# Batches 0 and 1 with one form of softmax, batch 1 divided after its product with V, masks as a transfer of their own, and a new listed order

## The chip, the cores and the metric

One core of one Trainium2 chip runs the whole kernel: TensorE (PE) for matmuls, VectorE (DVE), ScalarE (ACT) and GpSimd (POOL) for the element work, SyncE (SP) for issuing transfers. The metric is device microseconds of one execution; a median over several runs is given.

## What is computed

Attention with a sliding window over q, k, v of 8 batches, 8 heads, 576 positions and 64 features; heads 0 to 3 look at the 32 last positions, heads 4 to 7 at every fourth of the last 128. The 4,608 tokens x 512 features that come out go through a feed-forward layer whose activation is a quotient of polynomials.

```python
scores = scale * np.matmul(q, k.transpose(0, 1, 3, 2))        # q, k: (8, 8, 576, 64)
scores = np.where(masks, scores, -1e9)                        # window 32; heads 4..7 dilated by 4
attn = np.exp(scores - np.max(scores, axis=-1, keepdims=True))
attn = attn / (np.sum(attn, axis=-1, keepdims=True) + 1e-09)
x = np.matmul(attn, v).transpose(0, 2, 1, 3).reshape(8 * 576, 512)
h = x @ w_in                                                  # 512 -> 2048
P = a[0] + a[1] * h + a[2] * h**2 + a[3] * h**3
Q = 1.0 + np.abs(b[0]) * np.abs(h) + np.abs(b[1]) * h**2
out = (P / (Q + 1e-6)) @ w_out                                # 2048 -> 512
```

## The kernel before

**Feed-forward tiles.** PE's main work is 144 tiles, each of 512 tokens by 128 of the 2,048 hidden features (`Tile`, line 907). All operands are split in a high and a low part, so a product is three matmuls: a tile's h is 12 matmuls of 128x512 into one of two banks `h`, and its four outputs are 3 each, added up over 16 tiles in four banks `out`. In between lies a chain over the engines: |h| on ACT (`a`), Q's linear part `r`, the product `a<-r,a` on DVE or POOL, P by two DVE steps on `t`, the quotient by `ln` and `exp` on ACT (into the bank of h), three DVE products (`g1`, `g0`, `g2`, the last two on `a` and the bank), and the split into `gh` and `gl`. Tiles 0 to 7 are chunk 0 (batch 0's x), 8 to 23 chunk 1 (batch 1's x), 24 to 31 the rest of chunk 0, 32 on chunk 2. Weights arrive as 64-bit words and are converted on the core: scale on ACT, a low word on POOL or ACT, a join on DVE (`wi_f<-wi_f,wi_raw`), a high part and a low part (`wi<-wi_f,wi`).

**Attention.** 48 units n = 6 b + u run beside the tiles (`Unit`, line 382). A unit is 48 score matmuls into bank `pair`, a mask, a softmax, transposes, 48 products with V and the move of the results into x's layout, split into `xh` and `xl`. Batch 0 keeps its scores in bands and has banks `pair_A`, `pair_B` beside `pair`; batch 1 transposes by PE; both have the mask put into the bank by PE with a bf16 identity, ahead of the scores. From batch 2 on mask and transposes go over DVE and DRAM. Results of batches 1 on go by `y` to DRAM and back as `z`. `x0` must be whole before tile 0, `x1` before tile 8, `x2` before tile 32. The products of unit n use the bank in which the scores of unit n + 2 come next.

**Three forms of softmax.** `KIND` says which form a unit of batches 0 and 1 takes. Form 0: row maximum and subtraction on DVE, exp on ACT, sum, reciprocal on DVE, product on POOL or DVE. Form 1 (unit 4): six ACT instructions read the bank and sum up as well (`exp_bank`, line 451). Form 2 (units 6 to 11): DVE takes the negated maximum, PE adds it to the bank by two fp32 products with the identity (`sub_pe`, line 471; four matmul instructions), ACT reads the bank, and six ACT copies scale the result (`norm`, line 491). Units 4 and 5 form `xl0` by PE, which subtracts `xh0` in the bank by a negated identity (`less_hi`, line 631, with `LESS`).

**What sets the order.** Every operation is entered in `Plan` (line 127) with costs per engine and dependencies. `ORDER` (line 70) lists operation numbers in the order they are placed, with an engine's letter where it is chosen by hand; before, the list reaches about tile 30. What isn't listed is placed by `run` (line 195): the operation that can start first on any engine names the engine, and of those that can start there within 200 ns the one with the lowest due rank goes (`DUE`, `LATE`, `SLACK`). Instructions of an engine then run in that order. PE also gets some bf16 matmuls in its idle time at the very start (`keep_busy`).

Of the kernel before, what the change touches and what calls it, by code (L numbers as in the profile page):

```python
# [20 lines left out]
P = 128  # L21
# [5 lines left out]
BOTH = {"ACT": 375, "DVE": 465}  # L27
# [3 lines left out]
KIND = [0, 0, 0, 0, 1, 0] + [2] * 6  # L31
LESS = [0, 0, 0, 0, 1, 1]
# [246 lines left out]
def tile_attention_moe(  # L279
# [102 lines left out]
    class Unit:  # L382
# [280 lines left out]
        def plan(self, by, tags):  # L663
# [19 lines left out]
            if start:  # L683
                mask_users.append(sc)
# [582 lines left out]
```

## Time and profile before

| what | us |
|---|---|
| median of 3 runs (888.88 to 891.14) | 889.17 |
| the profiled execution's span | 887.4 |
| PE busy | 873.8 (98%) |
| DVE busy | 716.1 (81%) |
| ACT busy | 666.1 (75%) |
| POOL busy | 504.7 (57%) |
| first matmul of tile 0 | 35.78 |

The span is that of one profiled execution and is read for where time goes; the median is the time that counts. PE's granted clock is 1.0 in all stretches. Durations of matmuls overlap in the timeline, since they are pipelined, so the start of the next one is read rather than the end of one.

### The profile page before, as it was taken

Reading aid. Unit: us, or ns where it says so; the run is one execution under the profiler, and the core shown is the slowest. Engines: PE = TensorE matmul, PEld = TensorE weight load, DVE = VectorE, ACT = ScalarE, POOL = GpSimd, SP = SyncE. Lnnn points to the kernel's source line nnn. Section 1 sums busy time; section 2 is a strip of 40 time slices with the busy share of each in tenths; the row PEclk is TensorE's granted clock in tenths of the full one; section 3 lists DMA queues with packets and bytes.
Section 4 is the critical chain, followed back from the end, with each engine's and each line's share of the span. In section 5 each row is a group of like instructions: output and inputs, shape, how many; then the busy total and the mean of one; then the engine's idle time right before and its main releaser. Section 6 shows DMA issues by size and latency. Waiting matters only on the chain.

```text
span 887.4 us, 20762 instructions
## 1 busy us (share of the span) xinstructions
PE 873.8 (98%) x7991; PEld 710.8 (80%) x7991; DVE 716.1 (81%) x1280; ACT 666.1 (75%) x1108; POOL 504.7 (57%) x467
## 2 busy tenths in 40 slices
PE   7999999999999999999999999999999999999998
PEld 4777888888878888888888888888888888888886
DVE  6899999998899978878888788888766666667665
ACT  4999988776567877777767777767777788777773
POOL 4477867767555655556555464655554456444442
PEclk9999999999999999999999999999999999999999
DMA  9976451337534424433544344323310020001001
GB/s 345 346 247 205 178 216 31 106 110 229 168 121 131 139 76 149 135 113 115 157 144 140 107 133 163 113 90 98 119 27 1 1 71 1 1 1 48 1 1 47
DMA packets 85187, 102.64 MB, mean 116 GB/s; under 512 B 37216, under 2 KB 62560, under 8 KB 85088
## 3 DMA queue, kind: packets, MB, share of 16 engines
q1 hardware_dynamic: 85088, 101.32, 35.1%
q8 instruction: 62, 1.02, 0.5%
q14 instruction: 37, 0.30, 0.1%
HBM read 74.42 MB, written 26.87 MB: 114 GB/s over the span
## 4 chain that ended last, share of the span: by engine, by line
PE 90%; DVE 6%; ACT 1%; issue 1%; DMA 1%; POOL 0%; SPq 0%; DVEq 0%; ACTq 0%; POOLq 0%
PE out L337 43%; PE h L337 41%; PE pair L337 6%; DVE a L346 1%; DVE h L346 1%; DMA qk<-in_qk_dram 1%; ACT p L340 1%; DVE a L343 1%; DVE t L343 0%; DVE t L346 0%; DVE sm L485 0%; DVE y L567 0%; DVE wo_f L346 0%; DVE mx L445 0%; PE pair_B L337 0%
## 5 line engine op out<-in xcount | busy, mean ns | idle before, releaser
L337 PE MATMUL h<-xh,wi 128*128 128x512 f32 x1136 | 374.3, 391 | 1.5 <-DVE a L346 1.4
L337 PE MATMUL out<-gh,wo 128*128 128x512 f32 x1136 | 354.0, 393 | 0.0
L349 POOL TENSOR_TENSOR a<-r,a 128x512 f32<-128x512 f32 x130 | 168.6, 1297 | 232.1 <-ACT r L340 224.5
L337 PEld LDWEIGHTS h<-xh,wi 128*128 128x128 f32 x1136 | 213.2, 188 | 47.9 <-DVE a L346 2.5
L346 DVE SCALAR_TENSOR_TENSOR a<-a,h 128x512 f32<-128x512 f32 x280 | 191.2, 683 | 69.2 <-POOL gl L349 36.9
L337 PEld LDWEIGHTS out<-gh,wo 128*128 128x128 f32 x1136 | 210.6, 188 | 45.1
L337 PE MATMUL out<-gl,wo 128*128 128x512 f32 x568 | 221.3, 390 | 0.0
L337 PE MATMUL h<-xl,wi 128*128 128x512 f32 x568 | 221.2, 389 | 0.0
L349 POOL TENSOR_TENSOR gl<-a,gh 128x512 fp32r<-128x512 f32 x133 | 175.9, 1322 | 56.7 <-ACT gh L340 56.0
L340 ACT ACTIVATE a<-h 128x512 f32<-128x512 f32 x140 | 83.6, 597 | 104.7 <-PE h L337 101.9
L343 DVE TENSOR_TENSOR t<-t,h 128x512 f32<-128x512 f32 x142 | 97.2, 684 | 62.8 <-ACT t L340 62.0
L340 ACT ACTIVATE r<-a,ln_bias 128x512 f32<-128x512 f32 x141 | 100.9, 716 | 31.7 <-POOL a L349 27.4
L337 PEld LDWEIGHTS out<-gl,wo 128*128 128x128 f32 x568 | 106.7, 188 | 22.4
L337 PEld LDWEIGHTS h<-xl,wi 128*128 128x128 f32 x568 | 106.7, 188 | 21.9
L340 ACT ACTIVATE t<-h,na_t 128x512 f32<-128x512 f32 x142 | 108.5, 764 | 3.1 <-PE h L337 3.1
L340 ACT ACTIVATE h<-r,exp_bias 128x512 f32<-128x512 f32 x142 | 98.0, 690 | 16.7 <-DVE t L346 10.7
L346 DVE SCALAR_TENSOR_TENSOR t<-t,na_t,h 128x512 f32<-128x512 f32 x142 | 105.8, 745 | 4.2
L346 DVE SCALAR_TENSOR_TENSOR h<-t,na_t,h 128x512 f32<-128x512 f32 x142 | 106.1, 747 | 0.0
L340 ACT ACTIVATE r<-a,ab_t 128x512 f32<-128x512 f32 x120 | 97.9, 816 | 3.9
L340 ACT ACTIVATE gh<-a 128x512 fp32r<-128x512 f32 x130 | 81.8, 629 | 24.0 <-PE out L337 19.1
L349 POOL TENSOR_TENSOR xl<-z,xh 128x256 fp32r<-128x256 f32 (+5 forms) x60 | 44.1, 753 | 2.4 <-ACT xh L340 1.3
L349 POOL TENSOR_TENSOR p<-p,sm 128x384 f32<-128x384 f32 x36 | 30.7, 853 | 17.0 <-DVE sm L489 16.0
(131 smaller groups left out, 687.1 us busy)
## 6 DMA issues: line engine op xcount, KB each, us to landing
qk<-in_qk_dram SPq DMA_DIRECT2D x48, 448.0 KB, 5.0
v<-in_vp_dram SPq DMA_DIRECT2D x42, 384.0 KB, 3.8
out_dram<-os SPq DMA_DIRECT2D x36, 256.0 KB, 2.5
wi_raw<-in_w_in_dram SPq DMA_DIRECT2D x16, 512.0 KB, 7.6
wo_raw<-in_w_out_dram SPq DMA_DIRECT2D x16, 512.0 KB, 6.4
results<-y SPq DMA_DIRECT2D x42, 192.0 KB, 2.0
z<-results SPq DMA_DIRECT2D x168, 48.0 KB, 2.1
turned<-u SPq DMA_DIRECT2D x36, 192.0 KB, 2.0
```

What stands on the lines that cost most here:

```text
L337: pin(nc.tensor.matmul(o, lhs, rhs, start=start, stop=stop, skip_group_check=free))
L340: pin(nc.scalar.activation(o, i, func, **kw))
L343: pin(nc.vector.tensor_tensor(o, x, y, op))
L346: pin(nc.vector.scalar_tensor_tensor(o, x, s, y, op0, op1))
L349: pin(nc.gpsimd.tensor_tensor(o, x, y, op))
```

## The change

One form of softmax (0) stays. Batch 0's units keep sum, reciprocal and product; batch 1's units leave the sum and the division out (`defer`). V of batches 1 to 7 is stored with a 65th column of ones, so that the products give the sum of each row beside the result, and `rescale` divides in the bank, on DVE, before the results are turned. Masks and coefficients have a transfer of their own, `head_t`, from which they are read directly, and PE adds a mask behind the scores rather than ahead. PE no longer subtracts `xh0`; all of `xl0` comes from DVE. The biases of ACT are immediates instead of one-column tiles, and their memsets go. Most costs of the planner change by less than a fifth (the products of a unit of batch 0 from 1150 to 830 ns), and the list of operation numbers is another and reaches only to about tile 15.

```diff
-KIND = [0, 0, 0, 0, 1, 0] + [2] * 6
-LESS = [0, 0, 0, 0, 1, 1]
+VD = D + 1
 ORDER = """
-1 3 0 4 21 7 37 23 8 9 10 11 109 2 24 39 12 25 55 26 6 13d 110 14 16 27 28 29p 40 41 57 15a 42 32 58 43 17a 115 116 117p 18 19 139 30 111p 44 73 112
...
+2 3 5 1 7 0 8 9 10 21 37 55 11 12 23 4 24 121 73 13d 123p 39 25 40 16 57 14 41 22 26 17a 139 42 27 15a 28 122 29p 18 43 91 115 38 19 301 44 30 58 56
...
         def scores(self):
-            on_pe = self.on_pe
-            if on_pe:
-                for j, cnt, m in self.masks():
-                    ... mm(self.s[:, r, :192], ident_b, m[...], start=True, stop=False)
             for i in range(3):
                 for g in range(4):
                     for r in range(2):
...
+            if self.on_pe:
+                for j, cnt, m in self.masks():
+                    ... mm(self.s[:, r, :192], ident_b, m[...], start=False, free=True)
-        def exp_bank(self):
-            for j in range(6):
-                act(p[:, r, i], s[:, r, i], AF.Exp, bias=self.mx3[...], scale=0.125, accum_out=self.sm[...])
-        def sub_pe(self):
-            for r in range(2):
-                mm(self.s[:, r, :192], ident, mx, start=False, free=True)
         def norm(self, eng):
-            if eng == "ACT":
-                for j in range(6):
-                    act(self.p[:, j], self.p[:, j], AF.Copy, scale=self.sm[:, j : j + 1])
-                return
+        def rescale(self):
+            res = self.results()
+            t = att.tile([P, 18], F32, tag=plan.at("sm"), name=f"sm{self.n}")
+            sums, sm = (t[:, n : n + 6].rearrange("p (r i) -> p r i", r=2) for n in (6, 0))
+            pin(nc.vector.tensor_scalar(sums, res[:, :, :, D], 1e-9, None, ALU.add))
+            pin(nc.vector.reciprocal(sm, sums))
+            tt(res[:, :, :, :D], res[:, :, :, :D], sm.unsqueeze(3).to_broadcast([P, 2, 3, D]), ALU.mult)
         def turn_out(self):
+            if self.defer:
+                self.rescale()
-        def less_hi(self):
-        def copy_lo(self, eng):
...
+            mx = op({"DVE": 470}, 0, lambda e: self.max(), ma)
+            su = op({"DVE": 472}, 0, lambda e: self.sub(), mx, tail=-40)
+            ex = op({"ACT": 417}, 0, lambda e: self.exp(), su)
+            if not self.defer:
                 sm = op({"DVE": 465}, 0, lambda e: self.sum(), ex)
...
-            ln = op({"ACT": 660}, ... bias=ln_bias ...)
+            ln = op({"ACT": 535}, ... bias=GUARD * 2.0**-LOG_SHIFT ...)
+    head_t = const.tile([P, NMASK + 6], F32, name="head_t")
+    mask_t = head_t[:, :NMASK].bitcast(BF16).rearrange("p (m k) -> p m k", k=64)
```

How the order moves is shown at four pieces. Names carry the number of the unit or tile and, behind an underscore, of the buffer.

DVE just ahead of tile 0 (`xl0` is the low part of batch 0's x, `sm`, `mx` sums and maxima of a unit, `wi_f` a weight tile that is joined), before:

```order
L346 SCALAR_TENSOR_TENSOR wi_f2_467<-wi_f2_467,wi_raw2_440 128x512
L346 SCALAR_TENSOR_TENSOR wo_f0_520<-wo_f0_520,wo_raw0_445 128x512
L343 TENSOR_TENSOR wi0_413<-wi_f0_234,wi0_413 128x512
L485 TENSOR_REDUCE sm6_582<-p6_547 128x6
L488 TENSOR_SCALAR sm6_582<-sm6_582 128x3x2
L489 RECIPROCAL sm6_582<-sm6_582 128x6
L445 TENSOR_REDUCE mx7_590<-pair_85 128x6
L343 TENSOR_TENSOR wi2_543<-wi_f2_467,wi2_543 128x512
L343 TENSOR_TENSOR xl0_303<-pair_A_98,xh0_302 128x2x96
L343 TENSOR_TENSOR xl0_303<-pair_A_98,xh0_302 128x2x32
L343 TENSOR_TENSOR xl0_303<-pair_A_98,xh0_302 128x2x48
L346 SCALAR_TENSOR_TENSOR wi_f4_610<-wi_f4_610,wi_raw4_447 128x512
```

and with the change:

```order
L328 TENSOR_TENSOR xl0_303<-pair_A_95,xh0_302 128x2x32
L328 TENSOR_TENSOR xl0_303<-pair_A_95,xh0_302 128x2x48
L422 TENSOR_REDUCE mx7_594<-pair_85 128x6
L328 TENSOR_TENSOR p7_604<-pair_85,mx7_594 128x2x3x64
L331 SCALAR_TENSOR_TENSOR wi_f0_512<-wi_f0_512,wi_raw0_440 128x512
L337 COPY l5_664<-pair_A_95 128x2x16 x2
L328 TENSOR_TENSOR xl0_303<-pair_B_96,xh0_302 128x2x80
L328 TENSOR_TENSOR xl0_303<-pair_B_96,xh0_302 128x2x96
L328 TENSOR_TENSOR xl0_303<-pair_A_95,xh0_302 128x2x32
L328 TENSOR_TENSOR xl0_303<-pair_A_95,xh0_302 128x2x48
L328 TENSOR_TENSOR xl0_303<-pair_A_95,xh0_302 128x2x80
L1029 TENSOR_SCALAR na_t_93<-head_t_89 128x4
```

Five of the twelve rows of before are weight work (three of them joins) and three are a sum and its reciprocal; with the change one join is left in this place, and seven rows are pieces of `xl0`.

PE around the start of tile 1's h (`v7`, `qk9`: products of unit 7, scores of unit 9; `t8` the transposes of unit 8), before:

```order
L337 MATMUL h0_762<-xh0_302,wi0_413 128x512
L337 MATMUL pair_85<-v7_717,pT7_787 32x64 x24
L337 LDWEIGHTS ident_b_91
L337 MATMUL pair_85<-mask_t_89,ident_b_91 128x192
L337 LDWEIGHTS ident_b_91
L337 MATMUL pair_85<-mask_t_89,ident_b_91 128x192
L337 MATMUL pair_85<-qk9_699 32x64 x24
L521 MATMUL t8_850<-ident_90,p8_737 128x128 x3
L337 MATMUL pair_85<-mx9_854,ident_90 128x192 x2
L337 MATMUL h1_894<-xh0_302,wi1_371 128x512
```

and with the change:

```order
L322 MATMUL h0_700<-xh0_302,wi0_669 128x512
L473 MATMUL t8_731<-ident_90,p8_698 128x128 x3
L322 MATMUL pair_85<-v7_676,pT7_691 32x65 x24
L322 MATMUL pair_85<-qk9_689 32x64 x24
L322 LDWEIGHTS ident_b_91
L322 MATMUL pair_85<-head_t_89,ident_b_91 128x192
L322 LDWEIGHTS ident_b_91
L322 MATMUL pair_85<-head_t_89,ident_b_91 128x192
L322 MATMUL h1_819<-xh0_302,wi1_525 128x512
```

The masks moved from ahead of the scores to behind them, the products have 65 columns, and the two rows with `mx9` are gone.

PE at the end of tile 30's outputs, where batch 2's x comes in (`out0_1_8` is output 1 of chunk 0), before:

```order
L337 MATMUL out0_3_8_2914<-gh29_3343,wo13_2517 128x512 x2
L337 MATMUL out0_3_8_2914<-gl29_3346,wo13_2517 128x512
L337 MATMUL out0_0_8_2906<-gh30_3377,wo14_2634 128x512 x2
L337 MATMUL out0_0_8_2906<-gl30_3385,wo14_2634 128x512
L337 MATMUL h32_3414<-xh2_2759,wi0_413 128x512
L337 MATMUL h32_3414<-xl2_2760,wi0_413 128x512
L337 MATMUL h32_3414<-xh2_2759,wi0_413 128x512 x2
```

and with the change:

```order
L322 MATMUL out0_2_8_2840<-gh30_3242,wo14_2483 128x512 x2
L322 MATMUL out0_2_8_2840<-gl30_3256,wo14_2483 128x512
L322 MATMUL out0_3_8_2850<-gh30_3242,wo14_2483 128x512 x2
L322 MATMUL out0_3_8_2850<-gl30_3256,wo14_2483 128x512
L322 MATMUL out0_0_8_2822<-gh31_3279,wo15_2591 128x512 x2
L322 MATMUL out0_0_8_2822<-gl31_3285,wo15_2591 128x512
L322 MATMUL h32_3294<-xh2_2603,wi0_669 128x512
L322 MATMUL h32_3294<-xl2_2604,wi0_669 128x512
```

Tile 31's first output (`gh31`, `gl31`) stands ahead of h32 with the change; before, h32 and tile 30's other outputs, h33 and then `out0_0_8<-gh31` follow.

PE ahead of h34, which takes the bank of h32, with the change:

```order
L322 MATMUL h33_3321<-xl2_2604,wi1_525 128x512
L322 MATMUL h33_3321<-xh2_2603,wi1_525 128x512
L322 MATMUL out0_1_8_2831<-gh31_3279,wo15_2591 128x512 x2
L322 MATMUL out0_1_8_2831<-gl31_3285,wo15_2591 128x512
L322 MATMUL out0_2_8_2840<-gh31_3279,wo15_2591 128x512 x2
L322 MATMUL out0_2_8_2840<-gl31_3285,wo15_2591 128x512
L322 MATMUL out0_3_8_2850<-gh31_3279,wo15_2591 128x512 x2
L322 MATMUL out0_3_8_2850<-gl31_3285,wo15_2591 128x512
L322 MATMUL h34_3381<-xh2_2603,wi2_739 128x512
```

Between h33 and h34 stand three outputs; before, it was h32, three outputs, h33, four outputs and h34.

## Rows read from the trace of the kernel before

**Rows 1.** Page: the span; busy us, share, instructions of PE.

```profile
span 887.4 us, 20762 instructions
...
PE 873.8 (98%) x7991; PEld 710.8 (80%) x7991; DVE 716.1 (81%) x1280; ACT 666.1 (75%) x1108; POOL 504.7 (57%) x467
```

**Rows 2.** Stretches: length, busy (count) of PE, PEld, DVE, ACT, POOL, clock, DMA share, GB/s.

```profile
0.00:35.50 35.50, 28.10 (x662) 19.94 (x663) 27.49 (x67) 23.24 (x68) 16.15 (x30) 1.00 0.96 361
35.50:86.00 50.50, 48.60 (x671) 38.06 (x670) 48.49 (x89) 47.17 (x101) 35.31 (x38) 1.00 0.70 231
...
231.00:870.00 639.00, 638.56 (x5336) 523.48 (x5335) 494.88 (x872) 478.14 (x747) 346.59 (x300) 1.00 0.28 87
```

**Rows 3.** PE's timeline (start, us, what), then its waits, 0 to 90, 86 to 880.

```profile
41.23 0.92 PE L337 MATMUL pair<-mx,ident 128*128 128x192 f32 x4 [0.41 <-DVE mx L445]
41.85 0.53 PE L337 MATMUL h<-xh,wi 128*128 128x512 f32 x1
...
PE h L337 <- DVE a L346: 1.0, 2, 0.7
PE pair L337 <- DVE mx L445: 0.8, 2, 0.4
...
PE h L337 <- DVE a L346: 0.4, 1, 0.4
```

**Rows 4.** Groups of instructions, 0 to 90 us: count | busy us, mean ns | idle before.

```profile
L346 DVE SCALAR_TENSOR_TENSOR wi_f<-wi_f,wi_raw 128x512 int32<-128x512 int32 x10 | 8.3, 851 | 0.0
L349 POOL TENSOR_TENSOR wi<-wi_f,wi 128x512 fp32r<-128x512 f32 x5 | 7.3, 1464 | 0.1
L343 DVE TENSOR_TENSOR wi<-wi_f,wi 128x512 fp32r<-128x512 f32 x4 | 3.1, 778 | 0.0
L489 DVE RECIPROCAL sm<-sm 128x6 f32<-128x6 f32 x12 | 2.3, 192 | 0.4
L343 DVE TENSOR_TENSOR pair<-pair,mask_t 128x384 f32<-128x384 f32 x1 | 0.6, 558 | 0.0
```

**Rows 5.** PE's timeline at two of its stalls, and at tile 0's first matmul.

```profile
20.48 0.34 PE L337 MATMUL pair<-qk 64*32 64x64 f32 x13 [1.46 <-issue]
...
32.90 0.30 PE L337 MATMUL pair<-v,pT 64*32 64x64 f32 x2 [0.45 <-issue]
...
35.78 0.48 PE L337 MATMUL h<-xh,wi 128*128 128x512 f32 x1
```

**Rows 6.** Busy time by stretch, between the stalls and from the start.

```profile
14.00:20.45 6.45, 4.68 (x127) 3.69 (x127) 5.96 (x13) 4.65 (x15) 4.36 (x6) 1.00 1.04 400
20.45:32.85 12.40, 11.07 (x252) 8.54 (x251) 11.68 (x31) 11.34 (x37) 6.06 (x8) 1.00 1.02 385
...
0.00:11.90 11.90, 8.72 (x215) 4.93 (x218) 5.81 (x14) 3.49 (x6) 2.25 (x14) 1.00 0.83 298
...
0.00:25.30 25.30, 18.98 (x457) 12.85 (x458) 17.93 (x44) 13.83 (x37) 11.23 (x24) 1.00 0.93 353
```

**Rows 7.** Batch 1's x: PE's and POOL's timeline; the chain of waits there.

```profile
72.27 0.67 PE L337 MATMUL pair<-v,pT 64*32 64x64 f32 x44
...
83.47 1.36 POOL L349 TENSOR_TENSOR xl<-z,xh 128x64 fp32r<-128x64 f32 x2 [0.64 <-ACT xh L340]
...
83.50 5.44 PE h L337 x24
```

**Rows 8.** Timeline of the last tile: its first and its last steps.

```profile
870.05 0.60 ACT L340 ACTIVATE spare_h<-h 128x512 f32<-128x512 f32 x1 [0.94 <-PE h L337]
...
875.88 0.69 DVE L346 SCALAR_TENSOR_TENSOR spare_h<-spare_h,h 128x512 f32<-128x512 f32 x1
...
877.33 0.69 DVE L343 TENSOR_TENSOR gl<-spare_h,gh 128x512 fp32r<-128x512 f32 x1 [0.76 <-ACT gh L340]
```

**Rows 9.** Page: two of the costliest groups.

```profile
L349 POOL TENSOR_TENSOR a<-r,a 128x512 f32<-128x512 f32 x130 | 168.6, 1297 | 232.1 <-ACT r L340 224.5
...
L346 DVE SCALAR_TENSOR_TENSOR a<-a,h 128x512 f32<-128x512 f32 x280 | 191.2, 683 | 69.2 <-POOL gl L349 36.9
```

More of the change, by code (lines that the diff above doesn't have):

```diff
@@ L671, in plan @@
             if self.n == 0:
-                copies.append(op({"POOL": 500}, -30, lambda e: copy(e, mask_t, extra["mask"]), lv))
-                copies.append(op({"DVE": 80}, -30, lambda e: make_coefs(), lv, consts))
-                copies.append(lv)
-            masks = [copies[2 if start else 0], identity] if self.on_pe else []
+                copies.append(op({"SP": 430}, -30, lambda e: load(head_t, head), dma=(NMASK + 6) * 512))
+                copies.append(op({"DVE": 80}, -30, lambda e: make_coefs(), copies[0], consts))
+            masks = [copies[0], identity] if self.on_pe else []
             if len(Unit.open) >= DEPTH:
@@ L681, in plan @@
             else:
-                sc = op({"PE": 1000 + 150 * self.on_pe}, 0, lambda e: self.scores(), lq, *masks, words=96 + 4 * self.on_pe, tail=-100)
-            if start:
-                mask_users.append(sc)
+                sc = op({"PE": 800 + 120 * self.on_pe}, 0, lambda e: self.scores(), lq, *masks, words=96 + 4 * self.on_pe, tail=-100)
             if self.on_pe:
@@ L737, in plan @@
                 early.extend((lq, lv))
-            for o in (sc, ma, mx, su, ex, sm, rc, no, *(turns if start else [tr]), *self.placed, *([sb] if kind == 2 else [])):
+            for o in (sc, ma, mx, su, ex, *norms, *(turns if start else [tr]), *self.placed):
                 o.slack = 0.0
@@ L777, in finish @@
             if start:
[L778 to L786 removed]
+                el = op(low, 0, lambda e: self.evac_lo(e), eh)
                 if left:
[L788 removed]
+                    kl = op({"ACT": 172 + LEFT * 2, "DVE": 120 + LEFT * 2}, self.by + 1.0, lambda e: self.keep_left(e), av)
                     kept.append(kl)
@@ L807, in finish @@
                 plan.takes(self.placed[0], *(("p", PS) if self.n % 2 else ("pT", 1)), [av])
-            plan.takes(self.lv, self.vt, 1 if start else LOADS, [av] if self.n else [av, *copies[:2], *mask_users])
+            plan.takes(self.lv, self.vt, 1 if start else LOADS, [av])
             if b not in x_done:
@@ L852, in w_low @@
         if eng == "ACT":
[L853 removed]
+            act(low, low.bitcast(U32), AF.Identity, bias=LOW_BIAS, scale=LOW_SCALE)
         else:
@@ L969, in plan @@
             tail = i == NC * NF - 1
-            both = {"DVE": 602} if tail else {"DVE": 660, "POOL": 1290} if i < BOTH_TILES else {"POOL": 1290}
+            both = {"DVE": 602} if tail else {"DVE": 610, "POOL": 1270} if i < BOTH_TILES else {"POOL": 1290}
             h = op({"PE": 2740}, k, lambda e: self.h(), *x_done[c], *([w_done["wi", ft]] if c <= 1 else []), copies[1], words=24)
```

212 lines of the change are left out of this document (72 added, 140 removed).

## The prediction

> **What bounds the kernel now.** I read the busy times by stretch first: PE is 98% busy over the 887.4 us span, and in the long stretch from 231 to 870 us it works 638.56 of 639.00 [rows 1, 2]. After the first matmul of tile 0 at 35.78 PE is the bound almost everywhere, so a step of another engine is worth something only where PE waits for it. Those places are few. (1) The 35.78 us before tile 0, in which the transfers are full (0.96) and DVE, at 27.49 us busy, is nearly as full as PE [rows 2]. (2) Between tile 0 and about 90 us PE waits 1.0 for tile work (`DVE a`) and 0.8 for row maxima (`DVE mx`), and from 86 to 880 us 0.4 in all [rows 3]. (3) The first tiles of batch 1 (tile 8) and batch 2 (tile 32) need those batches' x; both come with hardly a wait now. So the time is start + PE's work + waits, and I cost the change as three such terms. The profiled execution's span is 887.4; the median of the runs is 889.17, 1.77 more, which I add at the end.
>
> **The start.** The softmax of batches 0 and 1, the low-part subtractions and the mask copy are rewritten here. Counted on DVE up to the last piece of `xl0`, the order has one maximum, one sum and two reciprocal pairs less, three subtractions more, four joins of weight words instead of seven, no weight low part instead of three, one copy instead of four, and twelve small pieces of `xl0` instead of seven. Three joins at 0.851 and three low parts at 0.778 [rows 4] are 4.9 us; the rest comes to some 1 us less: together -6 of the 27.49. DVE alone would let x0 stand whole at 29.5 to 31.1 (35.5 less 6, or less the 4.4 that are left if 1.6 of it falls where DVE waited). But something else holds PE too. It stands still with nothing that it waits for ("issue"): 1.46 us before 20.48 and 0.45 before 32.90, and once earlier, at 14.0 [rows 5]. Counted between these places, PE and its weight loads run 127 + 127 = 254 instructions from 14.00 to 20.45 and 252 + 251 = 503 up to 32.85 [rows 6]: one step of some 254, or two (a few records can be missing). So PE's instructions arrive in blocks of that size, about 256. When is one asked for? 433 had run at 11.90, and the block that begins with the 700th came at 20.48, 8.6 later; 457 + 458 = 915 had run at 25.30, and the one from about 1200 on came at 32.90, 7.6 later [rows 5, 6]. Taken as a delay of 7.6 to 8.6 behind an instruction some 300 earlier, this holds tile 0 (instruction 1325 or a few more now [rows 2], about 1310 in the new order): it lies behind that same block, and comes sooner only as far as the 915th runs sooner. In the new order the some 210 instructions from the stall at 20.48 up to there have no group of maxima on PE and fewer waits; I walked them at the matmuls' durations and put it at 23.2 (an estimate), the block at 30.8 to 31.8, and tile 0, 1.2 us of scores, transposes and products behind that, at 32.0 to 33.0. The last weight low part ahead of tile 0 (`wi0`) moves to POOL, 1.464 instead of 0.778 [rows 4], and ends at about the same time. I take 32.5: **-3.3**; bounds 0 (the stream doesn't get sooner) and -5.3 (DVE alone decides).
>
> **Batch 1's softmax.** What goes from behind tile 0: three groups of four fp32 matmuls `pair<-mx,ident`, the first at 41.23 with the next matmul, of tile 1, at 41.85, 0.62 later [rows 3], the others alike: **-1.9** of pure PE time. With them goes a wait of 0.8 for `mx`; but the new subtraction, exp and transposes run over DVE and ACT, whose place in front of a transpose is as long, and tile 2 still follows tile 0 closely (6.4 us of PE work between, 6.7 before). Of the 1.8 us of waits I count **-0.5**, bounds -1.8 and +1. ACT loses the 36 small copies `p<-p,sm`, some 9 us; ACT isn't waited for there, so that is worth nothing, and neither are immediates for the biases of `ln` and `exp`.
>
> **The division in the bank.** Each unit of batch 1 now has an add, a reciprocal and a 128x384 product in PSUM ahead of the turn: about 0.15 + 0.19 + 0.56 = 0.9 with hops 1.0 us, by the rows of the reciprocal and of the masked add of the same shape [rows 4]. While it runs the bank `pair` is held, with the next unit's scores and products behind it. For five of six units PE has tile work in between. The sixth decides: now the products of unit 11 start at 72.27, the last `xl` piece ends at 83.47 + 1.36 = 84.83, and tile 8, the second half of the 24 matmuls from 83.50, starts at 86.22 [rows 7]: trip 12.6, with 1.4 to spare. Afterwards the trip is 13.6 and PE has 14.2 us of work between (11 outputs, 2 h tiles and the scores; 12.9 before). On SP's queue, though, the read `z` of unit 11 stands behind two weight loads of 512 KB that weren't there; at the 361 GB/s of the first stretch [rows 2] they take up to 2.9 us. The wait is 0 to 2.3: **+1.0**. The 65th column is 1/64 of six products of 0.67: **+0.1**.
>
> **Tiles 31 to 34.** This is where I expect the loss. The list of numbers now ends at about tile 15, and the planner sets what follows. On PE, tile 31's first output stands right ahead of h32, with only the eight outputs of tiles 29 and 30, 5.4 us at 0.227 a matmul (5.44 for 24) [rows 7], behind h31; before, h32 and h33 lay in between, 18.1 us. And h34, which takes h32's bank, has h33 and three outputs ahead of it, 4.8 us, where the shortest such distance before was 6.7 (h0 to h2) and cost 0.3 (of the 1.0 for `DVE a`, 0.7 fell elsewhere) [rows 3]. What the chain of a tile takes with nothing in its way shows at the end: h has just ended at 870.05, the last product on `a` ends at 875.88 + 0.69 = 876.57, `gl` at 877.33 + 0.69 = 878.02 [rows 8], 6.5 and 8.0 us. The first two matmuls of an output need only `gh`, so PE stands at the third: with hops 8.1 + 0.23 against 5.3 + 0.68 (an output's three matmuls), **+2.4**; at h34 6.7 less 4.8: +1.9, say **+1.8**. The 0.4 of now [rows 3], in the same stretch of the work, is taken off: **+3.8** together. Lower bound 3; upper 8, if the chains go at 10.2 and 8.4. Batch 2's x hides in these stalls: its last two pieces on DVE stand behind `gl31`, and h32 behind tile 31's first output.
>
> The head of 99 KB instead of 355 lands sooner, but the masks are used behind the scores now, and `v0` is needed only by the first products; with the transfers full, nothing. POOL gets eight weight low parts by tile 7 (1.464 each) and gives off the masks' copy; it has room, 35.31 of 50.50 [rows 2].
>
> **Sum.** -3.3 - 1.9 - 0.5 + 1.0 + 0.1 + 3.8 = -0.8: span 886.6, and with 1.77 a time of 888.4.
>
> **The rivals.** *A, faster: the stream doesn't hold the start and tile 8 doesn't wait.* For it: the delay of a block differs from one to the next, and DVE is the fuller engine. Against it: PE stood at each of the blocks that the rows show. Tile 0 would come at 30.5, -2.0, and +1.0 falls away: 885.4. It takes 1.9 us below my sum to be faster by more than 0.3%.
>
> *B, slower: tile 31's and 32's chains are stretched.* In both, the product `a<-r,a` is on POOL, which takes 1.297 for it against 0.69 for a product of that shape on DVE [rows 8, 9], and DVE has `gl30` between tile 31's steps. With chains of 10.2 (the shortest distance that PE left a chain in the kernel before) instead of 8.0, and 8.4 for the bank instead of 6.5, the price is 2.2 + 1.9 = 4.1: 892.5. It decides from 3.4 us more than my sum. Against it: a PE that stands lets the others catch up. The joins, which read two SBUF tiles, take 851 beside POOL, the tile steps that read PSUM 683 [rows 4, 9]. The Trainium skill, "GPSIMD Engine Reference", section "Specifications", says that GpSimd shares its SBUF interfaces with VectorE, with contention for DVE instructions in a 2-port mode or with two SBUF inputs; by that rule eight more low parts on POOL would stretch the joins and `gl` on DVE and speak for B. The longer joins agree with it, though they differ in type as well, and no row here parts the two.
>
> *C, no gain at the start:* instruction 918 runs no sooner, tile 0 stays at 35.78, and only the rest counts: 891.7, just within what counts as no change.
>
> **How the numbers follow.** A measurement of this kernel tells 0.3% from no change, 2.7 us: faster is below 886.5, slower above 891.8. Forecast 0.43 and C 0.07, both within; A 0.28; B 0.22. So faster 0.28, same 0.50, slower 0.22. The range takes A and B in up to a tenth on either side: 884.5, a little below A's time (DVE alone deciding the start would give 886.4 by itself, and with no wait at tile 8 and -1.8 of waits 884.1), to 892.8, a little above B's.
>
> **What would show it.** In the profile of the changed kernel: tile 0 at 32.0 to 33.0, with an "issue" stall of PE some 1.2 us ahead of it (right: the stream; at 30.5 without such a stall: A; at 35.8: C). No `pair<-mx` on PE. A wait of 0 to 2.3 ahead of tile 8 on `xl`. Two waits of PE near 225 to 240 us, of about 2.4 in tile 31's first output for `gl` and 1.8 ahead of h34 for `DVE a`; both above 4, B. From 250 us on PE without waits as now; waits there that the order doesn't show, ahead of tile 48 above all, whose x has 14.9 us from its last unit's products (18.3 before), would make the prediction wrong.

## The result, and the profile after

The changed kernel takes 896.93 us (median of 4 runs, 896.29 to 898.57) against 889.91 for the kernel before in the same comparison: a ratio of 1.0081 (95% interval 1.0065 to 1.0097). It is slower by 7.0 us, outside the predicted range of 884.5 to 892.8. The profiled execution has a span of 894.5, 7.1 more than before, so its trace shows the loss.

The page's span and busy times, which answer to [rows 1]:

```profile
span 894.5 us, 20670 instructions
...
PE 874.0 (98%) x7969; PEld 705.2 (79%) x7969; DVE 727.5 (81%) x1298; ACT 631.6 (71%) x1067; POOL 497.4 (56%) x445
```

The same stretches as [rows 2], and one between them (length; busy us and count of PE, PEld, DVE, ACT, POOL; granted clock; DMA share; GB/s):

```profile
0.00:35.50 35.50, 29.07 (x670) 19.49 (x670) 26.18 (x64) 21.44 (x52) 13.45 (x23) 1.00 0.88 313
35.50:86.00 50.50, 46.77 (x651) 36.07 (x652) 48.28 (x90) 44.65 (x84) 39.04 (x37) 0.97 0.85 281
86.00:231.00 145.00, 141.20 (x1155) 113.65 (x1154) 137.60 (x231) 103.04 (x179) 97.19 (x88) 1.00 0.44 141
231.00:870.00 639.00, 636.13 (x5405) 519.12 (x5405) 502.44 (x897) 453.23 (x740) 341.73 (x295) 1.00 0.30 88
```

PE now stands for 3.7 us between 35.5 and 86, for 3.8 between 86 and 231, and for 2.9 in the long stretch, where it stood for 0.4. What it waits for (waits of PE, us in total, times, longest), first from 35.5 to 86, then from 86 to 880; these answer to [rows 3]:

```profile
PE pair L322 <- DVE y L535: 1.1, 1, 1.1
PE h L322 <- ACT pT L325: 0.7, 1, 0.7
PE h L322 <- ACT r L325: 0.7, 1, 0.7
PE t L473 <- DVE a L331: 0.7, 1, 0.7
...
PE h L322 <- DVE a L331: 3.6, 4, 1.6
PE out L322 <- DVE gl L328: 1.2, 2, 0.9
PE out L322 <- DVE gh L337: 0.9, 1, 0.9
PE out L322 <- POOL gl L334: 0.7, 1, 0.7
```

PE's timeline at the places that the prediction spoke of, and at those that it didn't (start, us, what, and in brackets the idle time before it): a stall with nothing to wait for and tile 0 ([rows 5]), the first wait for `y`, a wait for `pT`, tile 8's start ([rows 7]), then the stalls ahead of tile 16's low part in an output, of h19, of the same in tile 25's first output, of tile 31's first output and of h34:

```profile
19.15 0.41 PE L322 MATMUL pair<-qk 64*32 64x64 f32 x20 [0.92 <-issue]
...
31.49 0.48 PE L322 MATMUL h<-xh,wi 128*128 128x512 f32 x1
...
36.45 0.67 PE L322 MATMUL pair<-v,pT 64*32 64x65 f32 x44 [1.07 <-DVE y L535]
...
38.66 0.80 PE L322 MATMUL h<-xh,wi 128*128 128x512 f32 x1 [0.75 <-ACT pT L325]
...
85.48 0.43 PE L322 MATMUL h<-xh,wi 128*128 128x512 f32 x1
...
147.64 0.50 PE L322 MATMUL out<-gl,wo 128*128 128x512 f32 x1 [0.85 <-DVE gl L328]
...
151.78 0.50 PE L322 MATMUL h<-xh,wi 128*128 128x512 f32 x1 [1.58 <-DVE a L331]
...
203.89 0.50 PE L322 MATMUL out<-gl,wo 128*128 128x512 f32 x1 [0.69 <-POOL gl L334]
...
235.25 0.73 PE L322 MATMUL out<-gh,wo 128*128 128x512 f32 x2 [0.90 <-DVE gh L337]
...
245.56 0.50 PE L322 MATMUL h<-xh,wi 128*128 128x512 f32 x1 [1.48 <-DVE a L331]
```

Idle time is not all of it. By stretches, right behind the stall at 38.66 PE is busy but at a granted clock of 0.50, the lower of its two levels (1.2 GHz):

```profile
38.60:41.90 3.30, 3.24 (x8) 2.59 (x9) 3.20 (x9) 2.28 (x5) 3.30 (x4) 0.50 0.99 338
42.20:45.50 3.30, 3.30 (x108) 2.59 (x107) 2.11 (x4) 2.25 (x4) 1.62 (x3) 1.00 0.98 279
```

Eight 128x512 matmuls fill 3.3 us there, 0.43 each (1.06 us for two that follow one another), where one takes 0.227 otherwise: some 1.6 us lost that no wait shows. It isn't by itself what makes the kernel slow: of the four executions, the one whose mean granted clock is 1.000 (the others have 0.998) takes 897.56.

**A balance from tile 0 on.** To compare kernels whose tile 0 starts at different times, I took each profile's order on PE and added up what its instructions take at full clock without waits (0.227 a 128x512 matmul, 0.66 for 48 products or scores, and so on). Time passed since tile 0's first matmul, less that sum, is what was lost. Before needs 840.6 us of such work behind tile 0's start, the changed kernel 838.6. The loss up to the start of the products of units 8, 12, 13, 17 and 18, and up to PE's end (the start of its last matmul and 0.227):

| kernel | tile 0 | unit 8 | 12 | 13 | 17 | 18 | end | PE ends |
|---|---|---|---|---|---|---|---|---|
| before | 35.78 | 1.0 | 4.3 | 4.4 | 4.6 | 4.7 | 7.1 | 883.46 |
| after | 31.49 | 4.2 | 8.7 | 12.4 | 13.8 | 17.9 | 20.6 | 890.68 |
| b_short_list | 35.07 | 1.0 | 4.4 | 5.0 | 7.2 | 11.9 | 17.8 | 893.44 |
| a_costs_b | 31.69 | 2.0 | 6.5 | 7.4 | 9.9 | 15.0 | 17.3 | 888.59 |
| a_no_divide | 31.76 | 1.7 | 6.4 | 10.1 | 11.5 | 15.5 | 18.1 | 888.45 |
| a_h20_b | 33.44 | 4.3 | 10.2 | 14.0 | 14.1 | 14.6 | 17.6 | 889.67 |
| a_all_b2 | 38.56 | 4.6 | 12.4 | 12.6 | 12.7 | 12.9 | 16.2 | 893.38 |
| c2_seam | 32.38 | 3.1 | 6.6 | 7.2 | 7.3 | 7.4 | 10.1 | 882.38 |

Matmuls that the planner put in PE's idle time behind tile 0's start count as work here, 0.25 each: 1.0 us in a_costs_b and 1.3 in c2_seam, nearly all of it ahead of unit 12. With them, these two lose 7.5 and 7.6 up to unit 12.

So the +7.2 at PE's end are: start -4.3, work -2.0, and 13.5 more lost: 4.4 up to unit 12, 3.6 from there to unit 13 (the stalls at 147.64 and 151.78), 1.2 to unit 17 (the one at 203.89), 4.0 to unit 18 (tiles 31 to 34), 0.3 behind. A stall costs some 0.2 to 0.3 more here than its idle time, since the matmul ahead of it counts as busy beyond 0.227 and the one behind it takes 0.34.

### The profile page after: what moved, and what is told of

Read it like the earlier page. It is cut to its first block, busy times and chain, and to the rows that moved or that the text cites. A ratio compares the mean times of both kernels' runs of the same rounds, so it can differ in the third digit from the quotient of the medians.

```text
span 894.5 us, 20670 instructions
## 1 busy us (share of the span) xinstructions
PE 874.0 (98%) x7969; PEld 705.2 (79%) x7969; DVE 727.5 (81%) x1298; ACT 631.6 (71%) x1067; POOL 497.4 (56%) x445
## 4 chain that ended last, share of the span: by engine, by line
PE 84%; DVE 10%; issue 2%; ACT 2%; POOL 1%; DMA 0%; SPq 0%; DVEq 0%; POOLq 0%; ACTq 0%
PE out L322 39%; PE h L322 39%; PE pair L322 5%; DVE a L331 2%; DVE h L331 1%; DVE wi_f L331 1%; DVE t L328 1%; PE pair_A L322 1%; DVE wo_f L331 1%; DVE mx L422 1%; DVE gl L328 1%; DVE t L331 1%; DVE sm L441 0%; PE pair_B L322 0%; ACT t L325 0%
## 5 line engine op out<-in xcount | busy, mean ns | idle before, releaser
L322 PE MATMUL h<-xh,wi 128*128 128x512 f32 x1136 | 376.1, 392 | 5.4 <-DVE a L331 3.6
L322 PE MATMUL out<-gh,wo 128*128 128x512 f32 x1136 | 355.7, 394 | 1.3 <-DVE gh L337 0.9
L334 POOL TENSOR_TENSOR a<-r,a 128x512 f32<-128x512 f32 x137 | 178.0, 1299 | 245.3 <-ACT r L325 221.7
L322 PEld LDWEIGHTS h<-xh,wi 128*128 128x128 f32 x1136 | 213.9, 188 | 55.1 <-DVE a L331 7.4
L322 PEld LDWEIGHTS out<-gh,wo 128*128 128x128 f32 x1136 | 210.4, 188 | 47.9 <-DVE gh L337 1.3
L322 PE MATMUL out<-gl,wo 128*128 128x512 f32 x568 | 221.7, 390 | 2.0 <-DVE gl L328 1.2
L322 PE MATMUL h<-xl,wi 128*128 128x512 f32 x568 | 221.9, 391 | 0.0
L334 POOL TENSOR_TENSOR gl<-a,gh 128x512 fp32r<-128x512 f32 x129 | 169.1, 1311 | 30.9 <-ACT gh L325 30.1
L322 PEld LDWEIGHTS out<-gl,wo 128*128 128x128 f32 x568 | 106.6, 188 | 26.7 <-DVE gl L328 2.5
L322 PEld LDWEIGHTS h<-xl,wi 128*128 128x128 f32 x568 | 107.1, 189 | 21.8
L325 ACT ACTIVATE r<-a 128x512 f32<-128x512 f32 x141 | 88.1, 625 | 41.1 <-POOL a L334 39.1
L325 ACT ACTIVATE h<-r 128x512 f32<-128x512 f32 x142 | 85.3, 601 | 23.8 <-DVE t L331 15.9
L325 ACT ACTIVATE gh<-a 128x512 fp32r<-128x512 f32 x127 | 79.9, 629 | 29.4 <-PE out L322 21.4
L334 POOL TENSOR_TENSOR xl<-z,xh 128x256 fp32r<-128x256 f32 (+5 forms) x52 | 39.0, 765 | 7.8 <-ACT xh L325 7.6
```

The source lines that it names most:

```text
L322: pin(nc.tensor.matmul(o, lhs, rhs, start=start, stop=stop, skip_group_check=free))
L325: pin(nc.scalar.activation(o, i, func, **kw))
L334: pin(nc.gpsimd.tensor_tensor(o, x, y, op))
```

## The experiments

Two theories. **The order:** the edits themselves are not what costs; the listed order is shorter, and what the planner puts behind it makes PE wait. **The edits:** the division in the bank, and more weight work beside DVE's own, cost time wherever they stand. Kernels that start with a are the changed kernel, with b the kernel before. In kernels with a whole list the program's lines stand about 100 further down (L422 is L322 of the changed kernel).

**Only the list of before cut short.**

```diff
 ORDER = """
-(1117 entries, to about tile 30)
+(the first 677 of them, to tile 14's first output)
```

> The kernel before, with nothing changed but the length of its list: it ends at tile 14's first output, as the list of the changed kernel does, and the planner with the costs of before sets the rest. Theory 1 (order): the end of the list alone costs several us: 893 to 901, with PE waits behind `DVE a` and `gl` between 140 and 260 us, none before. Theories 2 and 3: 889.5 to 891, no new waits.

It took 899.63, a ratio of 1.0113 (1.0097 to 1.0129): the kernel before loses 10.5 us by its list's end alone, with nothing else changed. Waits of PE from 86 to 880 us:

```profile
PE h L325 <- DVE a L334: 6.6, 7, 2.6
```

They are of the kind that the changed kernel shows, seven instead of one; the largest stands at the same place in the work, ahead of h34, with the clock at 0.50 behind it (PE's timeline, then two stretches):

```profile
243.53 0.50 PE L325 MATMUL h<-xh,wi 128*128 128x512 f32 x1 [2.59 <-DVE a L334]
...
244.70:248.10 3.40, 3.40 (x10) 2.63 (x9) 2.48 (x4) 0.72 (x2) 3.40 (x4) 0.50 0.73 232
248.50:251.90 3.40, 3.40 (x107) 2.63 (x106) 2.52 (x4) 2.78 (x5) 0.30 (x1) 1.00 0.44 155
```

The loss begins only behind unit 12, where the list ends; up to there the balance is that of before.

**The division left out.**

```diff
         def turn_out(self):
-            if self.defer:
-                self.rescale()
```

> The changed kernel with the division of batch 1's results in the bank left out (the add, the reciprocal and the 128x384 product of six units are not done, so batch 1's attention is not normalised); order and all else unchanged. 6 x 1.0 us of DVE work go from the stretch of tiles 0 to 8. Theory 2 (the division holds the bank and loads DVE): PE's wait of 1.1 us at 36 us for `y` goes and the waits between tile 0 and tile 8 fall by half, 3 us or more: 892 to 894. Theory 1 (order): only the wait at 36 us goes, and part of it comes back: 895.5 to 896.5.

895.81, ratio 1.0073 (1.0058 to 1.0088): 1.1 us less than the changed kernel by the medians, with overlapping intervals. Up to unit 8 it loses 1.7 instead of 4.2; the wait for `y` and the stretch at half clock are gone, but part of it comes back as a wait for the transfer of V (PE's waits, 32 to 90 us):

```profile
PE pair L322 <- DMA v<-in_vp_dram: 1.9, 2, 1.3
PE h L322 <- ACT pT L325: 1.0, 1, 1.0
```

From unit 12 on it loses what the changed kernel loses (11.7 and 11.9), so the division is not the cause there. Up to unit 12 it loses 2.3 less, of which the stretch at half clock is 1.6.

**The planner's costs for weights and tiles as they were.**

```diff
-            jn = op({"DVE": 605}, ...)
+            jn = op({"DVE": 640}, ...)
-        lo = op({"DVE": 605, "POOL": 1300}, ...)
+        lo = op({"DVE": 660, "POOL": 1450}, ...)
-            both = {"DVE": 602} ... {"DVE": 610, "POOL": 1270} ...
+            both = {"DVE": 602} ... {"DVE": 660, "POOL": 1290} ...
-            ln = op({"ACT": 535}, ...)      # and ex 537, ab 497, ql, gh, lw, hi
+            ln = op({"ACT": 660}, ...)      # and ex 615, ab 515, ...
```

> The changed kernel with the planner's costs of the kernel before for the weights and the tiles (gl, joins, ln and others some 5 to 20 per cent dearer); its list is the same, so the order moves only behind tile 15. Theory 1a (the cheaper costs make the planner place chains too tightly): fewer waits between 150 and 250 us, 892 to 894. Theory 1b (what counts is that there is no list, whatever the costs): 896 to 900, the waits at other places.

895.15, ratio 1.0070 (1.0053 to 1.0088), between the two ranges that were expected. The loss from unit 12 to 13 shrinks from 3.7 to 0.9, so it hangs on the order that the lower costs gave; but others grow. There are again four waits for `DVE a`, and the one ahead of h34 is now 2.58:

```profile
PE h L322 <- DVE a L331: 4.4, 4, 2.6
```

**The changed kernel's edits with an order written out to the end.** Here the list covers the whole program: to a tile's h it is the changed kernel's own, and from there on that of before. In one of them it is that of before from the first instruction.

```diff
 ORDER = """
 ...
-1188 1189a 1200 400 1201 397p 1199p 1202 1203 208 1221 1190d 198d 1222 409 201p ...
+1188 1189a 1200 400 1201 397p 1199p 1202 1203 208 1221 201p 409 212 214 365 ...
```

(a_order_b; in the others the two lists part at another entry, and `BUSY_UNTIL` goes from 150000 to 30000, which takes away bf16 matmuls that the planner put in PE's idle time: 17 in a_order_b, 4.3 us at 0.25 each.)

To tile 8's h its own, with these matmuls:

> The changed kernel with all its edits, but from tile 8's h on every engine takes its operations in the order that the kernel before has (same engines, too); up to there it is unchanged. Theory 1 (order): the stalls of PE behind tile chains between 100 and 250 us of the changed kernel (111, 124, 147, 151, 204, 235, 245 us; some 7 us with their restarts) come from the order alone, so the time falls by 5 to 7 to 890 to 892, and PE waits under 2 us between 86 and 260 us. Theory 2 (the softmax puts more work on DVE, which then lags): the stalls stay, 896 to 897. Theory 3 (the half clock and the start of tile 0 to 8 are all): 896 to 897, too.

892.65, ratio 1.0042 (1.0025 to 1.0059): 4.3 less than the changed kernel, a little short of the 5 to 7. Without them:

> All edits of the change and its own order up to tile 8's h, from there the order of the kernel before, and without the 17 idle-time matmuls (bf16, 128x512, 0.25 us each, 4.3 us) that the planner put into PE's queue between tiles 0 and 16 in a_order_b. Theory 1 (order, and those matmuls are pure cost): 888 to 890, the loss of PE between the start of tile 0 and the end some 11 to 12 us (before 7.1, changed kernel 20.6). Theory 1b (they only filled time in which PE would have waited): 891.5 to 892.5, PE waits longer by the same 3 to 4 us at these places.

893.5, ratio 1.0051 (1.0036 to 1.0066), above both ranges and no better: they had only filled time in which PE would have waited. Where 14 of them stood, at 89 us, its profile has waits of 1.3 for `wo` and 1.2 for `gl`, and a granted clock of 0.50 from 93.1 to 96.3. To tile 20's h its own:

> The changed kernel with its own order up to tile 20's h, from there the order of the kernel before: this takes away only the places at tile 31's first output and at h34 (and those close by), and leaves the stalls at 146 and 150 us. Theory 1 with the size of my prediction: the losses at 204, 231, 234 and 244 us go, 4 us: 892 to 893.5, and those at 146 and 150 us (2.8) stay. Theory 2 (a lag of DVE that any order shows): the losses move on, 895.5 to 897.

894.3, ratio 1.0055 (1.0038 to 1.0071), between the two ranges: the loss of tiles 31 to 34 falls from 4.1 to 0.5, and 2.6 us of the 7.0 are gone, while the pair of stalls of the changed kernel's list is still there (PE's timeline):

```profile
151.26 0.50 PE L422 MATMUL out<-gl,wo 128*128 128x512 f32 x1 [0.83 <-DVE gl L428]
155.41 0.50 PE L422 MATMUL h<-xh,wi 128*128 128x512 f32 x1 [1.58 <-DVE a L431]
```

In the order of before throughout:

> All edits of the change in the order of the kernel before from the first instruction on (each new operation at the place of the one whose work it takes: the subtraction on DVE where PE added the maxima, the division ahead of the turn; no idle-time matmuls behind tile 0). Theory 1 (order): tiles 8 to 40 lose no more than before, PE has 2.0 us less to do, tile 0 starts at 33 to 36, and the time is 887 to 892. Theory 2 (the new softmax by itself delays the tiles of batches 0 and 1): 4 us or more lost between tile 0 and tile 8 beside the 3 of before: 892 to 896.

898.09, ratio 1.0100 (1.0083 to 1.0117), above both ranges. With the old order the edits do cost, at the front: tile 0 starts at 38.56, 2.8 later than before, and up to unit 12 it loses 12.4 against 4.3. From there to unit 18 it loses no more than before (0.5 and 0.4). PE waits ahead of tile 0 for a piece of `xl0` behind weight work on DVE:

```profile
35.51 0.88 PE L422 MATMUL pair_A<-turned_bands,v 128*64 128x96 f32 x16 [1.51 <-DVE xl L428]
```

A part of it may be the clock, which was low for 6.6 us ahead of tile 0 (a stretch of the profile; the four executions have mean clocks of 0.992 to 0.996). No run takes that part away.

```profile
21.20:27.80 6.60, 6.03 (x52) 3.91 (x53) 4.22 (x11) 2.63 (x7) 1.76 (x2) 0.50 1.03 404
```

**The best of both.** The order that the dearer costs gave (a_costs_b) up to tile 18's or tile 17's h, from there on that of before:

> All edits of the change; up to tile 18's h the order that the planner makes with the dearer costs (that of a_costs_b: own list, then placed without the list), from there the order of the kernel before; no idle-time matmuls behind 30 us. In a_costs_b PE had lost 7.4 us by unit 13's products (changed kernel 12.4), 17.3 in the end; the order of the kernel before adds 2.7 to 4 from there. Theory 1 (order alone decides behind tile 8, and the stalls of 147 and 151 us and of tiles 31 to 34 are two separate places of the planner): a loss of 10.5 to 12, the end 6 us sooner than in a_costs_b, 888 to 890, level with the kernel before. Theory 2 (time won early is given back by any order, as DVE is full): 892 to 894.

> The same with the seam one tile earlier (tile 17's h), which moves some of the weight work of tiles 18 to 20. Theory 1: within 1 us of c_h18_b, 888 to 890. Theory 2: 892 to 894.

891.29 and 891.27, ratios 1.0023 (1.0013 to 1.0032) and 1.0025 (1.0014 to 1.0035), between the two ranges. Both have one new stall, my own slip: where the two lists meet, the stores of four outputs stood in another sequence than the copies ahead of them, so that an output's bank came free late (PE's timeline of the first):

```profile
106.61 0.72 PE L422 MATMUL out<-gh,wo 128*128 128x512 f32 x2 [1.71 <-ACT os L425]
```

a_h20_b has the same wait, 1.71 at 108.82, and is too slow by it. a_order_b and a_h8_b2 have no wait for `os`; what they lose where their own lists meet, at tile 8's h, is told above. So all of these tell by the places of their losses, not by their totals. Mended, in c_h18_b's order:

```diff
-BUSY_UNTIL, ... = 30000.0, ...
+BUSY_UNTIL, ... = 150000.0, ...
-... 387 1258 1248 388 202 ...
+... 387 1258 1248 1218 388 202 ...
-... 1563 453 1564 1571 1509a 1510 476 1572 ...
+... 1563 453 1516 1564 1571 1509a 476 1572 ...
```

(the other stores of the same kind likewise; 1.3 us of idle-time matmuls come back with it.)

> As c_h18_b, with one slip of that order taken out: at the seam it had the stores of the four outputs of chunk 0's first half in another sequence than the copies that feed them, so that an output bank came free late (PE's wait of 1.7 us for `os` at 104 us, with restart 1.9). Theory 1 (order alone behind tile 8): 889 to 889.7, the wait at 104 us is gone and the loss falls from 13.5 to about 11.5. Theory 2 (DVE is full, so what is won is waited for later): 891 as c_h18_b, the wait appears at another place before unit 13's products.

888.61 against 889.01, ratio 0.9998 (0.9988 to 1.0007): level with the kernel before. All edits of the change are in it. From 86 to 880 us PE waits for 0.8 in all:

```profile
PE h L422 <- DVE a L431: 0.8, 3, 0.3
```

**Two of its early waits moved.** Batch 1's first division goes ahead of a weight's join on DVE, and a copy of `pT` ahead of a weight's high part on ACT.

```diff
-... 1069 327 160 320 108 145 ... 154 131p 1074 155a ... 333 329a 1076 ...
+... 1069 327 320 160 108 145 ... 154 131p 1074 329a 155a ... 333 1076 ...
```

> As c2_seam, with two more places changed between tiles 0 and 1: on DVE unit 6's division and turn go ahead of the join of `wo_f3` (0.68 us), on ACT the copy of unit 8's transposes goes ahead of the high part of `wi4` (0.63 us). PE waits there 1.1 us for `y` and 0.7 for `pT`, ahead of unit 7's products and of tile 1's h, in the changed kernel and in all that share its first 80 us. Theory 1 (the waits between tile 0 and tile 8 are order, too): both waits fall by 0.6, the end 1 us sooner than c2_seam. Theory 2 (the division itself makes them): they fall by 0.2 or less, or come back as waits before tile 8, the same time as c2_seam.

889.39, ratio 1.0000 (0.9990 to 1.0011): nothing. The wait for `y` halves from 1.1 to 0.5, but PE then stands for V's transfer (its waits, 33 to 90 us; c2_seam waits 1.2 for it), and behind that its clock stays at 0.50 for 6.6 us of the profile, which is of the slowest of the twelve executions:

```profile
PE pair L422 <- DMA v<-in_vp_dram: 1.9, 1, 1.9
PE h L422 <- ACT r L425: 0.8, 1, 0.8
PE pair L422 <- DMA qk<-in_qk_dram: 0.6, 1, 0.6
PE pair L422 <- DVE y L635: 0.5, 1, 0.5
...
44.60:51.20 6.60, 5.95 (x75) 4.57 (x68) 6.39 (x13) 4.76 (x9) 6.37 (x6) 0.50 0.99 335
```

At this place of the profile the transfers (share 0.99) are the next limit. No version here beats the kernel before.

**What follows.** The order theory holds behind unit 12, where 9.1 of the 13.5 us were lost: the cut list alone slows the kernel before by 10.5 us, and c2_seam, with all the edits and a better order, loses there only 0.7 more than before and is level with it. The other 4.4 fell up to unit 12. c2_seam still has 2.3 of them, 3.3 with its idle-time matmuls, and the earlier start pays for that. How much of this is the edits and how much the new list's front stays open. That the edits can cost there shows in the old order, in which the new DVE steps delay tile 0 and the tiles up to unit 12.

## Why the prediction was wrong

Term by term, predicted and measured at PE's end: the start -3.3 and -4.3; work -1.8 and -2.0; waits up to unit 12, tile 8's among them, +0.5 and +4.4; tiles 31 to 34 +3.8 and +4.0; all else nothing and +5.1. So the step that failed is that PE would wait elsewhere as now, which the sum took without a reason, though the planner had placed all of that anew; behind it comes the term of the waits up to unit 12, too small by 3.9.

**The start: right in size, by luck.** Tile 0 came at 31.49, just outside the 32.0 to 33.0. Ten of the profiles (this one, and those of all experiments but b_short_list and a_all_b2) have the same instructions in the same order up to there, and their tile 0 lies between 31.49 and 33.44, 32.5 on average, the value taken; a single profile scatters by 1 us. But the reason given, that PE's instruction stream holds tile 0 by the block ahead of it, isn't borne out: PE stands with nothing to wait for before 19.15, but not ahead of tile 0, and the block that was to come at 30.8 to 31.8 brought its instructions with no stall. Of the ten, a_no_divide alone has the stall that was foretold, and only 0.30 of it. What PE waits for last ahead of tile 0 is DVE, 1.4 us for `turned_bands` at 25.82; the price of that wait wasn't in the sum. It is the earlier stall, near 20 us, that goes with the start: in five of the ten it is 0.92 and tile 0 comes at 31.49 to 32.38, in the other five 1.71 to 1.89 and tile 0 at 32.58 to 33.44. (PE's timeline of a_h20_b, then of a_no_divide.)

```profile
21.08 0.41 PE L422 MATMUL pair<-qk 64*32 64x64 f32 x20 [1.89 <-issue]
...
30.66 0.25 PE L322 MATMUL pair<-v,pT 64*32 64x65 f32 x2 [0.30 <-issue]
```

**The maxima: right.** No group `pair<-mx` is left, and the work behind tile 0 is 2.0 less (predicted 1.9 less, and 0.1 more for the 65th column).

**Tile 8: wrong by 1.0, harmless.** It starts at 85.48 with no wait; the last piece of `xl` had ended at 84.90 (POOL's timeline):

```profile
83.54 1.36 POOL L334 TENSOR_TENSOR xl<-z,xh 128x64 fp32r<-128x64 f32 x2 [1.31 <-ACT xh L325]
```

**The waits up to unit 12: the first mis-sized term.** -0.5 was taken, -1.8 and +1 were the bounds; the loss grew by 4.4. The prediction let waits change places but not multiply. There are four of 0.7 to 1.1 where there were two sorts of 0.8 and 1.0 in all, of which a wait for `y` (the divided and turned results, 1.1) is new. And a stall brought the lower clock, 1.6, which the sum didn't price: the kernel before had stalls of at most 0.7 in this place [rows 3] and no such stretch. Without it the growth is smaller: a_costs_b and c2_seam have the same order up to unit 12, but for their idle-time matmuls, and no such stretch, and lose 3.2 and 3.3 more than before with these matmuls. The term of 1.0 for the division looked at the sixth unit, since PE has tile work beside the others; the wait came at the first, at 36.45, where batch 1's first results are divided while tile 0 has only just begun.

**Tiles 16 to 19: the step that failed.** "Waits there that the order doesn't show" was named as what would make the prediction wrong, but for the stretch from 250 us on. The sum had nothing for units 12 to 17 (122 to 221 us), and 4.8 were lost there, 3.6 of it at tiles 16 to 19. It had priced a place only where PE's order left a chain less than it takes at the end of the program, 8.0. Tile 16's distance is long enough for that: h17, h18 and twelve outputs lie between, and its h ends at 132.57, 14.2 us before its low part is wanted. But its chain takes 15.0, to 147.58. Here is DVE's timeline, then POOL's, at 136 to 148 us; `gl` at 137.42 is tile 15's, the two `a<-a,h` and `gl` at 146.92 are tile 16's:

```profile
137.42 1.78 DVE L328 TENSOR_TENSOR gl<-a,gh 128x512 fp32r<-128x512 f32 x1
139.12 1.78 DVE L328 TENSOR_TENSOR wo<-wo_f,wo 128x512 fp32r<-128x512 f32 x1
140.82 0.67 DVE L331 SCALAR_TENSOR_TENSOR a<-a,h 128x512 f32<-128x512 f32 x1
...
142.19 0.69 DVE L331 SCALAR_TENSOR_TENSOR a<-a,h 128x512 f32<-128x512 f32 x1
...
146.92 0.66 DVE L328 TENSOR_TENSOR gl<-a,gh 128x512 fp32r<-128x512 f32 x1
...
136.90 1.75 POOL L334 TENSOR_TENSOR wo<-wo_f,wo 128x512 fp32r<-128x512 f32 x1
138.61 1.74 POOL L334 TENSOR_TENSOR wi<-wi_f,wi 128x512 fp32r<-128x512 f32 x1
...
143.17 1.29 POOL L334 TENSOR_TENSOR wi<-wi_f,wi 128x512 fp32r<-128x512 f32 x1 [2.82 <-ACT wi L325]
```

Tile 16 stands behind a low part of a weight, and at its own end behind steps of tile 17 and of a softmax. h19 waits at 151.78 in the same way for `a` of tile 17, with a join and a high part ahead of it on DVE. DVE isn't overloaded, it is badly arranged: c2_seam has it equally busy in this stretch, and PE stands for 0.48 instead of 3.8 (stretch 86 to 231 us of c2_seam):

```profile
86.00:231.00 145.00, 144.52 (x1264) 117.08 (x1263) 136.74 (x244) 109.89 (x190) 103.59 (x98) 1.00 0.49 152
```

So these stalls belong to the planned order; a_costs_b, too, cuts the loss there, from 3.7 to 0.9.

**Tiles 31 to 34: right in place, partly by luck in size.** 3.8 predicted (two stalls, with 0.4 taken off), 4.0 lost, as three stalls of 0.33 (tile 30's first output), 0.90 (tile 31's first, for `gh31` where `gl31` was foretold) and 1.48 (h34, foretold at 1.8), with what a stall costs beyond its idle time, which the sum didn't have: the idle time alone is 2.7, and the larger of the two stalls that were foretold, 2.4 at tile 31's first output, was 0.90. a_h20_b, with the order of before here, loses 0.5.

**The rivals.** A's two conditions came true, no stall of the stream right ahead of tile 0 and no wait at tile 8, and the time was still slower: neither decided. B had the sign, but at the wrong tiles. Its mechanism is in the rows at 137 to 141 us: with POOL on steps of two SBUF tiles beside them, DVE's two steps take 1.78 each, where tile 16's `gl` takes 0.66, and POOL's 1.75 and 1.74 instead of 1.29. Their ends read as turns taken: 138.65 on POOL, 139.20 on DVE, 140.35 on POOL, 140.90 on DVE. On tile 16's chain that is some 2.2 us, more than the stall of 0.85. The joins of `wi_f` in the first 90 us average 1106 ns where [rows 4] had 851, with POOL doing eight low parts of `wi` beside them instead of five (groups of the changed kernel, 0 to 90 us); those of `wo_f` hardly moved, from 869 to 882:

```profile
L334 POOL TENSOR_TENSOR wi<-wi_f,wi 128x512 fp32r<-128x512 f32 x8 | 10.2, 1286 | 1.5 <-ACT wi L325 1.3
L331 DVE SCALAR_TENSOR_TENSOR wi_f<-wi_f,wi_raw 128x512 int32<-128x512 int32 x8 | 8.7, 1106 | 0.0
```

The Trainium skill, "GPSIMD Engine Reference", section "Specifications", states contention for DVE instructions with two SBUF inputs; the trace agrees. The prediction found no row that parts this from the type of the steps, but the traces do, step by step: in the changed kernel joins with no two-input step of POOL beside them average 772 ns, those with one beside them for half of their time or more 1156, while the steps `a<-a,h`, which read PSUM, take 685 and 683. But the kernel before stretches such steps as well: there joins take 690 and 1076, and `gl` on DVE has a mean of 1025 ns, 939 in the changed kernel. In each of the two kernels 24 steps of DVE (joins, `gl`, low parts of weights and `a<-r,a`) have POOL beside them like that. So it isn't the difference between the two kernels as a whole. That it makes the stall at 147.64 is argued, not shown: no run kept the order and took away the contention.

**C** fell with the start. The chances put 0.78 on faster or the same. The order behind the list was treated as two places with a price, though it is nine tenths of the tiles, and all of it had been placed anew.

## What to carry to other kernels

When a hand-made order gets shorter, the part that a planner now fills is the change: price it as a whole, by looking where each chain runs through a busy engine, and try it alone (the old kernel with its list cut) before pricing the edits. Time won ahead of the first tile is kept only if the order behind it keeps it; here 6.3 us won in start and work ended as a loss of 7. Price a stall of the bound engine at more than its length where the clock may drop behind it.

## What the runs showed of the hardware

- Behind some stalls of 0.8 to 2.6 us PE's granted clock was 0.50 for 3.3 to 6.6 us (rows above), at some 1.6 us lost for 3.3; behind others as long (1.58 at 151.78, 1.48 at 245.56 in the changed kernel) it stayed at 1.00. Between 30 and 880 us it was at 0.50 nowhere in the profiles of the kernel before and of c2_seam, which are level, nor in those of c_h18_b and a_no_divide, which are slower. It differs from one execution of a kernel to the next: of c3_swaps' twelve, the five with a mean granted clock of 1.000 took 887.69 to 889.16 us, the four with 0.996 took 889.62 to 891.34.
- DVE's and POOL's steps with two SBUF inputs, side by side, took up to 2.7 and 1.35 times as long as otherwise (1.78 and 0.66 us; 1.74 and 1.29). On average DVE's joins took 1156 ns beside such a step of POOL and 772 without, in the changed kernel.
- The same instructions up to tile 0, in the same order on PE and DVE, started it anywhere from 31.49 to 33.44 us. The five starts up to 32.38 had a stall of PE of 0.92 near 20 us with nothing to wait for, the five later ones 1.71 to 1.89.
